# A lent fourth PSUM bank, later casts and a later batch 1 in a kernel of clustered attention and four experts

## The chip, the cores and the metric

The kernel runs on one core of one Trainium2 chip. The metric is the device time of one execution in microseconds (us). "Span" is the time from the first to the last recorded instruction of a profiled execution; it is about 1.8 us shorter than the device time. Engines are named as in the profile: PE is TensorE's matmuls, PEld its weight loads, DVE VectorE, ACT ScalarE, POOL GpSimd, SP the engine that issues most DMAs. The program gives each engine its own queue of instructions and makes engines wait for each other by semaphores; in the traces here an engine takes its queue in order (in pair 2 of the kernel before, an eviction that could have run at 175.7 us stood behind two casts until 178.32). PSUM is the memory that PE writes its sums to, in banks.

## The reference

Four batches, eight heads, 768 positions, head dimension 64. Queries and keys are put into one of 16 clusters per head, and attention is allowed only inside a cluster. The result goes through four experts, each a two-layer network, weighted by given probabilities.

```python
q_assign = np.argmax(np.einsum('bhsd,hcd->bhsc', q_n, c_n), axis=-1)
k_assign = np.argmax(np.einsum('bhsd,hcd->bhsc', k_n, c_n), axis=-1)
mask = q_assign[:, :, :, None] == k_assign[:, :, None, :]
scores = np.where(mask, scale * np.matmul(q, k.transpose(0, 1, 3, 2)), -1e9)
...                                        # softmax, then times v
x = attn_out.transpose(0, 2, 1, 3).reshape(3072, 512)
p = domain_probs / (domain_probs.sum(-1, keepdims=True) + 1e-09)
for e in range(4):                         # w1[e]: 512x1024, w2[e]: 1024x512
    h = np.maximum(x @ w1[e], 0.0)
    out += p[:, e:e + 1] * (h @ w2[e])
```

## The kernel before

The order of instructions is written by hand: a list of attention steps is woven with the expert matmuls of positions that are already done, and generators prepare the next batch (its "assignment": transposes, cluster scores, one-hots) at given step numbers. There are 72 attention steps to a batch (PER_B). The eight PSUM banks are shared out by tag:

```python
PS_BUFS = {"s": 2, "av": 1, "av2": 1, "mo": 3, "misc": 1}
def bank(tag, dtype=F32):
    n = 512 if dtype == F32 else 1024
    return psum.tile([128, n], dtype, name="ps_" + tag, tag=tag, bufs=PS_BUFS[tag])
```

A tile of a tag that is in use waits until its bank has been evicted. Three kinds of tile take "mo": the experts' hidden tiles (evicted by ACT), the experts' outputs (evicted by DVE), and the cluster scores of batches 2 and 3 (evicted by DVE).

```python
def expert(u, e):
    ...
        ph = bank("mo")
        ...  nc.tensor.matmul(ph[...], W1[e][...], xT[...], ...)          # L728
        nc.scalar.activation(ht, ph, ACT.Relu)                            # L734
    ...
        po = bank("mo")[:, c]
        ...  nc.tensor.matmul(po, hT[...], W2[e][...], ...)               # L747
        nc.vector.scalar_tensor_tensor(oacc[:, c], po, pap, oacc[:, c],   # L756
                                       op0=ALU.mult, op1=ALU.add)
```

The assignment of batches 2 and 3 handles four tiles (z = 0 is the first of two, z = 1 the second). Scores come in pairs, each of two groups of four fp32 matmuls, which the trace records as eight: a pair for each half of the heads, so pairs 1 and 2 belong to batch 2, pairs 3 and 4 to batch 3.

```python
        def casts(self):                       # DVE, two of 0.95 us per tile
            ...  dve(self.rows(...), self.all[...])                      # L387
        def scores_split(self, bank_tag):
            sc = bank(bank_tag)
            ...  nc.tensor.matmul(sc[32 * x:32 * x + 32, :QW], lhs, rhs, ...)   # L400
            ...  dve(self.sch[...], src[...])                            # L404
        ...
                t = 8 * y
                    put(t + 9 + j, lambda x=x, j=j: x.merge(j))          # POOL, L377
                put(t + 15, x.casts)
                at = 16 * (y // 2) + 24
            if b == 1:
                ...
            put(at, lambda x=x: x.scores_split("mo"))
            put(at + 2 + 6 * z, x.cross_scores)
            put(at + 5 + 6 * z, x.merge_scores)                          # POOL, L416
```

Batch 1 is prepared in another way, with transposes on PE into the single "misc" bank (L242), at the very start:

```python
    for b in range(1, B):
        gens.append(Paced(assigns(b), XSTEPS[b], PER_B * (b - 1) if b > 1 else S1 + 4,
                          PER_B * b - 2))
```

The softmax here doesn't subtract the row's maximum and nothing guards it: scores larger than these inputs give would overflow.

## Time and profile before

| | before |
|---|---|
| median of the first three runs | 482.76 us (482.57 to 483.82) |
| span | 480.9 us |
| PE busy | 467.7 us, 97% |
| DVE, ACT, POOL busy | 47%, 58%, 39% |
| granted TensorE clock in the profiled run | 1.0 throughout |

PE is the bound, and 13.2 us of its span are idle. The question is which of these the change can take. The lines that answer it (the table of what PE waited for, the windows by expert period and the timelines around the gaps) stand in the prediction. Read there: a line of a timeline is start, length, engine, source line, operation, output and inputs, count; in square brackets the idle time ahead of it and the instruction that ended it.

### The profile page before, as it was taken

To read this page: it belongs to the slowest core of one execution; us is meant where nothing else is said; L and a number is where in the kernel's file an instruction comes from. 1 tells how busy PE (TensorE), PEld (TensorE's weight loads), DVE (VectorE), ACT (ScalarE), POOL (GpSimd) and SP (SyncE) were. 2 spreads that over 40 slices of the span, in tenths; PEclk is the share of its full clock that TensorE was granted. 3 is DMA by queue.
4 is the path that set the end of the run, shared out by engine and by line. 5 is a ranking of instruction groups with operands and counts; after the bars stand their busy time and mean duration, and the time that the engine had idled before them with its cause. 6 is when DMAs were issued, how large, how long until landed. Compare 5 with 4: busy or idle time off the path is not lost.

```text
span 480.9 us, 11389 instructions
## 1 busy us (share of the span) xinstructions
PE 467.7 (97%) x4539; PEld 332.6 (69%) x4539; DVE 226.7 (47%) x561; ACT 277.4 (58%) x502; POOL 186.2 (39%) x301
## 2 busy tenths in 40 slices
PE   8998999999999989999999999999999999999997
PEld 4776777677775657767766776777666666766675
DVE  5864664222324562422234444431877867765112
ACT  5755656555564546656655665566566585574341
POOL 5937479273343667180145834000313222221000
PEclk9999999999999999999999999999999999999999
DMA  8999953824564743614565573312000100100101
GB/s 281 254 211 347 237 106 54 152 57 127 92 131 111 159 102 81 143 34 51 140 140 110 119 135 115 87 35 75 27 29 13 50 14 7 34 30 10 46 2 44
DMA packets 74557, 48.01 MB, mean 100 GB/s; under 512 B 50248, under 2 KB 69256, under 8 KB 74504
## 3 DMA queue, kind: packets, MB, share of 16 engines
q1 hardware_dynamic: 65256, 37.96, 31.8%
q0 software_dynamic: 8576, 9.25, 10.8%
q8 instruction: 35, 0.57, 0.5%
q10 hardware_dynamic: 672, 0.08, 0.1%
q14 instruction: 18, 0.15, 0.1%
HBM read 37.31 MB, written 6.30 MB: 91 GB/s over the span
## 4 chain that ended last, share of the span: by engine, by line
PE 85%; DMA 5%; DVE 3%; SPq 3%; POOL 2%; issue 1%; ACT 0%; POOLq 0%; DVEq 0%; ACTq 0%
PE ps_mo L728 32%; PE ps_mo L747 31%; PE ps_s L638 8%; PE ps_av L665 7%; DMA raw<-in_k_dram 4%; SPq L368 1%; PE ps_s L548 1%; DMA sct<-scs 1%; SPq L336 1%; PE ps_misc L242 1%; POOL t L377 1%; PE ps_mo L400 1%; PE ps_mo L242 1%; PE ps_misc L548 1%; DVE oacc L756 1%
## 5 line engine op out<-in xcount | busy, mean ns | idle before, releaser
L644 ACT ACTIVATE at<-ps_s 128x512 bf16<-128x512 f32 x252 | 147.9, 595 | 125.7 <-PE ps_s L638 110.5
L728 PE MATMUL ps_mo<-xT,w1b 128*128 128x256 bf16 (+1 forms) x1664 | 195.7, 264 | 0.0
L747 PE MATMUL ps_mo<-w2b,hT 128*128 128x512 bf16 (+1 forms) x776 | 189.9, 377 | 2.8 <-DVE oacc L756 2.8
L728 PEld LDWEIGHTS <-w1b 128*128 128x128 bf16 x1664 | 146.3, 98 | 24.1 <-issue 0.6
L734 ACT ACTIVATE hT<-ps_mo 128x512 bf16<-128x512 f32 x192 | 114.7, 598 | 60.7 <-PE ps_mo L728 57.6
L756 DVE SCALAR_TENSOR_TENSOR oacc<-ps_mo,psb,oacc 128x512 f32<-128x512 f32 (+1 forms) x73 | 54.2, 742 | 125.5 <-PE ps_mo L747 125.3
L747 PEld LDWEIGHTS <-hT 128*128 128x128 bf16 x776 | 67.2, 98 | 61.4 <-issue 6.6
L638 PE MATMUL ps_s<-qf,kf 80*128 80x256 bf16 (+1 forms) x456 | 82.8, 267 | 0.7 <-DVE t L252 0.4
L665 PEld LDWEIGHTS <-at 128*128 128x128 bf16 x1152 | 69.9, 97 | 15.3 <-issue 1.7
L665 PE MATMUL ps_av<-vx,at 128*128 128x65 bf16 x1152 | 80.3, 193 | 0.0
L651 POOL TENSOR_TENSOR at<-at,same 128x512 bf16<-128x512 bf16 x24 | 28.2, 1176 | 97.7 <-ACT at L644 82.2
L638 PEld LDWEIGHTS <-kf 80*128 80x128 bf16 x456 | 42.4, 98 | 20.7 <-issue 1.6
L565 DVE TENSOR_SCALAR same<-qf,late 128x256 bf16<-128x256 bf16 x144 | 39.1, 324 | 0.0
L377 POOL COPY t<-t 128x768 uint16<-128x768 uint16 x32 | 35.6, 1119 | 0.3 <-DMA t<-h 0.3
L651 DVE TENSOR_TENSOR at<-at,same 128x512 bf16<-128x512 bf16 x48 | 21.6, 451 | 25.9 <-ACT at L644 25.8
L358 POOL COPY h<-raw 128x768 uint16<-128x768 uint16 x16 | 13.0, 826 | 37.2 <-DMA raw<-in_q_dram 31.0
L754 DVE TENSOR_SCALAR oacc<-ps_mo,psb 128x512 f32<-128x512 f32 x18 | 13.5, 750 | 28.5 <-PE ps_mo L747 28.5
L361 POOL COPY h<-raw 128x768 uint16<-128x768 uint16 x16 | 13.0, 825 | 33.0 <-DMA raw<-in_q_dram 19.5
L336 POOL DMA_DIRECT2D kf<-oht x32 | 16.4, 526 | 22.9 <-DMA oht<-oh 14.2
L416 POOL COPY st<-sct 128x384 uint16<-128x384 uint16 x16 | 9.9, 662 | 37.5 <-DMA sct<-scs 37.2
L672 DVE RECIPROCAL zr<-ps_av 128x4 f32<-128x4 f32 (+1 forms) x50 | 8.9, 178 | 30.1 <-PE ps_av L665 30.0
L674 DVE TENSOR_TENSOR xn<-ps_av,zr 128x256 bf16<-128x256 f32 (+1 forms) x50 | 20.7, 414 | 1.7
(127 smaller groups left out, 284.8 us busy)
## 6 DMA issues: line engine op xcount, KB each, us to landing
raw<-in_v_dram SPq DMA_DIRECT2D x8, 768.0 KB, 5.6
out_dram<-oacc SPq DMA_DIRECT2D x23, 256.0 KB, 2.0
raw<-in_k_dram SPq DMA_DIRECT2D x7, 768.0 KB, 6.6
raw<-in_q_dram SPq DMA_DIRECT2D x6, 768.0 KB, 4.9
w1b<-in_moe_w_dram POOLq DMA_DIRECT2D x4, 1024.0 KB, 11.8
w2b<-in_moe_w_dram POOLq DMA_DIRECT2D x4, 1024.0 KB, 17.1
qf<-nos SPq DMA_DIRECT2D x2, 768.0 KB, 4.0
xT<-xn SPq DMA_TRANSPOSE x72, 2.4
```

Of the source, the lines that this page charges most:

```text
L336: (nc.gpsimd if self.b or self.i0 and self.g else nc.sync).dma_start(out=self.rows(slice(D, D + CL), j, r), in_=self.oht[p0:p0 + CL, :self.w])
L377: pool(self.all[:, y * w:(y + 1) * w].bitcast(U16)[:, z::2], self.t16[:, (2 * z + y) * w:(2 * z + y + 1) * w])
L565: nc.vector.tensor_scalar(same[:, x * 256:(x + 1) * 256], clusters(b)[:, g, w, k // 2, k % 2, :], key_nos[b % 2][:, g, 8 * i + 4 * (k // 2 ...
L638: nc.tensor.matmul(sp[:, x * n:(x + 1) * n], KF[b % 2][:K, h, r, i * 128:(i + 1) * 128], QF[b % 2][:K, h, rs[0]:rs[-1] + 1, w * 128:(w + 1 ...
L644: nc.scalar.activation(at, sp, ACT.Exp, scale=scale)
L651: (nc.gpsimd if n4 in POOL_STEPS else nc.vector).tensor_tensor(at, at, same_cluster(b, w, cur), op=ALU.mult)
L665: nc.tensor.matmul(av[:, h % 2, m, :], at[:, c0:c0 + 128], VX[b % 2][:, h, 2 * i + r, :], start=(first and x == 0 and m == 0), stop=(last ...
L674: nc.vector.tensor_tensor(xn[:, :nr].rearrange("p i j d -> p j i d"), av[:, :, :, :D], zr.broadcast_to([128, 2, nr, D]), op=ALU.mult)
L728: nc.tensor.matmul(ph[:, x * n:(x + 1) * n], W1[e][:, i, (f + x) * 128:(f + x + 1) * 128], xT[:, i, :], start=(i == 0), stop=(i == ND - 1))
L734: nc.scalar.activation(ht, ph, ACT.Relu)
L747: nc.tensor.matmul(po, hT[f // per][:, c0:c0 + 128], W2[e][:, f, c], start=(f == 0), stop=(f == NF - 1))
L756: nc.vector.scalar_tensor_tensor(oacc[:, c], po, pap, oacc[:, c], op0=ALU.mult, op1=ALU.add)
```

## The change

Its intent: give the crowded places a fourth bank, keep long DVE work from standing ahead of evictions, and start batch 1's preparation when its key load has landed. It has three parts.

```diff
+    spare, turns = False, 0
+    def ring():
+        nonlocal turns
+        turns += 1
+        return bank("misc" if spare and turns % 4 == 0 else "mo")
...
-        def scores_split(self, bank_tag):
-            sc = bank(bank_tag)
+        def scores_split(self):
+            sc = ring()
...
-                put(t + 15, x.casts)
+                put(t + 15 + 4 * z, x.casts)
...
-            put(at, lambda x=x: x.scores_split("mo"))
+            put(at, x.scores_split)
...
-            ph = bank("mo")
+            ph = ring()
...
-                po = bank("mo")[:, c]
+                po = ring()[:, c]
...
-        gens.append(Paced(assigns(b), XSTEPS[b], PER_B * (b - 1) if b > 1 else S1 + 4,
-                          PER_B * b - 2))
+        gens.append(Paced(assigns(b), XSTEPS[b], PER_B * (b - 1) if b > 1 else S1 + 7,
+                          PER_B * b - (2 if b > 1 else -2)))
...
+                spare = PER_B + 4 <= step < PER_B * (B - 1)
```

"misc" is lent between steps 76 and 216, when batch 1's transposes, its main user, are done. In the changed kernel all source lines below stand eight lines further down: L747 becomes L755, L756 becomes L764, L400 becomes L408, L242 becomes L250, L377 becomes L385, L387 becomes L395, L416 becomes L424.

More of the change, by code (lines that the diff above doesn't have):

```diff
@@ L894 @@
     for b in range(1, B):
-        gens.append(Paced(assigns(b), XSTEPS[b], PER_B * (b - 1) if b > 1 else S1 + 4,
-                          PER_B * b - 2))
+        gens.append(Paced(assigns(b), XSTEPS[b], PER_B * (b - 1) if b > 1 else S1 + 7,
+                          PER_B * b - (2 if b > 1 else -2)))
     def woven(works, upto):
+        nonlocal spare
         base, spent = step, 0.0
```

## The prediction

> **What bounds the kernel now.** I read the page's first part, then the table of who waited for whom with TensorE (PE) alone, then PE's timeline from end to end, then the timelines of VectorE (DVE), GpSimd (POOL) and the DMA queue (SP) around each gap in it.
>
> ```profile
> PE 467.7 (97%) x4539; PEld 332.6 (69%) x4539; DVE 226.7 (47%) x561; ACT 277.4 (58%) x502; POOL 186.2 (39%) x301
> ...
> PE ps_mo L747 <- DVE oacc L756: 2.8, 2, 2.0
> PE ps_misc L242 <- DMA raw<-in_k_dram: 2.0, 2, 1.6
> ...
> PE ps_mo L400 <- DVE oacc L756: 1.0, 1, 1.0
> PE ps_misc L242 <- DVE t L252: 0.5, 2, 0.3
> ```
>
> PE is idle 480.9 - 467.7 = 13.2 us of the span. A busy PE need not be a full one, so I checked the rate. Late in the chain, where experts run alone:
>
> ```profile
> 442.82 3.49 PE ps_mo L728 x32
> 446.31 3.45 PE ps_mo L747 x16
> ```
>
> That is 109 ns for a matmul of 256 columns and 216 ns for one of 512. In the middle of the kernel one expert period holds 32 of L728, 16 of L747, 12 of L638 (256 columns) and 24 of L665 (65 columns). The first three need 3.49 + 3.45 + 12 x 0.109 = 8.25 us, and the period is 9.01, which leaves 32 ns for each L665. So PE is at its pace there, and a fourth bank has nothing to take from an ordinary period. Four periods also hold a pair of score groups (L400). The windows below are, in order: ordinary, score pairs 1 to 4, ordinary. Columns: stretch, length, then busy us of PE, PEld, DVE, ACT and POOL.
>
> ```profile
> 129.83:138.84 9.01, 9.01 (x85) 6.59 (x84) 3.83 (x6) 5.56 (x10) 0.55 (x1) 1.00 0.76 168
> 138.84:150.60 11.76, 10.76 (x101) 6.85 (x100) 5.97 (x10) 5.56 (x10) 6.44 (x8) 1.00 0.51 81
> 168.62:181.19 12.57, 10.59 (x101) 7.06 (x100) 8.35 (x14) 5.56 (x10) 8.53 (x13) 1.00 0.47 115
> 253.26:263.80 10.54, 10.54 (x101) 6.92 (x100) 5.02 (x9) 5.56 (x10) 5.50 (x7) 1.00 0.60 100
> 281.82:293.29 11.47, 10.60 (x102) 7.00 (x100) 7.78 (x14) 5.56 (x10) 5.98 (x8) 1.00 0.44 55
> 302.30:311.31 9.01, 9.01 (x86) 6.59 (x85) 4.05 (x9) 5.56 (x10) 0.00 (x0) 1.00 0.28 41
> ```
>
> Pair 3 loses nothing (PE busy all of 10.54 us), so a pair costs 10.54 - 9.01 = 1.53 us of real work. The others should then also take 10.54, and lose 11.76 - 10.54 = 1.22, 12.57 - 10.54 = 2.03 and 11.47 - 10.54 = 0.93 us: 4.18 us together. The worst one, PE first and then DVE:
>
> ```profile
> 175.12 0.59 PE L747 MATMUL ps_mo<-w2b,hT 128*128 128x512 bf16 x2
> 175.65 1.50 PE L400 MATMUL ps_mo<-t,bdc 128*32 128x384 f32 x16
> 179.13 1.02 PE L747 MATMUL ps_mo<-w2b,hT 128*128 128x512 bf16 x4 [1.98 <-DVE oacc L756]
> ...
> 175.16 0.98 DVE L426 TENSOR_SCALAR oh<-oh 128x384 bf16<-128x384 bf16 x1
> 176.07 2.22 DVE L387 CAST qf<-t 64x1536 bf16<-64x1536 f32 x2
> 178.32 0.75 DVE L756 SCALAR_TENSOR_TENSOR oacc<-ps_mo,psb,oacc 128x512 f32<-128x512 f32 x1
> ```
>
> The ring "mo" has three banks. The first output of the expert, score group A and score group B fill all three within 2 us; the second output (L747 at 179.13) needs the first one's bank. Its eviction L756 could have run at about 175.7, but stood in DVE's queue behind the one-hot work and the two casts until 178.32. Pair 1 is alike, except that score group B is the one that waits, and the casts themselves waited for POOL's last merge (ended 145.29).
>
> The other stall of note is before batch 1's first transposes:
>
> ```profile
> 41.13 0.52 PE L242 MATMUL ps_misc<-ident,raw 128*128 128x128 f32 x3 [1.62 <-DMA raw<-in_k_dram]
> ...
> 45.54 0.55 PE L242 MATMUL ps_misc<-ident,raw 128*128 128x128 f32 x3 [0.34 <-DVE t L252]
> ```
>
> The load of that key tile was issued at 33.25 and landed at 41.0; PE came to it at 39.5. A third small one (0.18 us, at 59.9) is again a transpose waiting for the copy out of the single "misc" bank.
>
> **What the Trainium skill says.** "PSUM — Partial Sum Buffer", Specifications (TRN2): eight banks of 2 KiB a partition, so no ninth can be had. The kernel's pools take 2 + 1 + 1 + 3 + 1 = 8; the fourth has to be lent. "Perfetto Trace Analysis", Matmuls: independent groups should rotate through different banks, so that the eviction of one overlaps the next one's matmuls. The ordinary periods agree with three banks (9.01 of 9.01 us busy); the pairs show three run out. The same page, Identifying the Most-Contended Engine: matmul busy share is no good measure of closeness to the roof, hence my check by pace. "TensorE: Matmul & The Clock Gate", Back-to-back issue gap: N / 2.4 + 2.5 ns, which is 109 and 216 ns for 256 and 512 columns. The trace agrees to a nanosecond; the sustained 131 ns that the section names for 512 columns is not seen here.
>
> **The change, part by part.** It adds and removes no instruction. I compared the built programs: POOL's and SP's orders are identical, DVE's has the casts moved, and PE's has batch 1's transposes and scores moved; otherwise only bank names change.
>
> Fourth bank. From step 76 to 216 every fourth allocation of the expert and score matmuls takes "misc". In the built program pair 1 has first output, second output, A, B on banks 3, 2, 4, misc, and pairs 2 and 4 have first output, A, B, second output on 3, 4, 2, misc: four different banks each time. What held misc before is an expert hidden tile four allocations back, which ACT evicts in 0.6 us, so no wait replaces the old one. The next user of the first output's bank is the following expert's first tile, some 4 us later in pair 1 and 3.5 us in pair 2; L756 then has that long. Worth the 4.18 us in full.
>
> Casts. Those of each second tile move four paced steps later, behind the score copies and the next evictions. They last 2 x 0.95 us on DVE, which is 47% busy, and their data is needed only in the next batch. By themselves they would take most of the same stalls away; together with the bank the gain isn't counted twice. So 0 beyond the 4.18. They make it safer: in pair 1 L756 no longer queues behind a cast that waits for POOL.
>
> Batch 1 three steps later. In the new PE order three attention steps with two L747 each, some 0.77 us a piece, come ahead of the first transpose: 39.5 + 3 x 0.77 = 41.8, after the landing at 41.0. The 1.62 us go. The transposes are then less bunched on misc, so the 0.34 and 0.18 should go also: 2.14 at most. Against that, the last transposes and back-transposes move into steps where matmuls of an expert on "mo" stand closer. Going through the bank numbers by hand I find one tight place: a hidden tile reuses the bank of the one before it but for 0.8 us of other work, against 0.6 us of ACT plus its start, up to 0.3 us. I take 1.9 us net.
>
> Sum: 4.18 + 1.9 = 6.1 us; 482.76 - 6.1 = 476.7 us, ratio 0.987.
>
> **The rivals.** First: PE only trades the bank wait for a wait on POOL. Scores need the merged tiles. In pair 1 the last merge ends at 145.29 and group B starts about 0.75 us after 146.31, a margin of 1.8 us; in pair 2 it ends at 176.03 and group B starts near 176.4, a margin of 0.4 us. If the loads and DMA transposes didn't move forward with PE, the gain of pairs 2 and 4 would go: about 479.5 us. Against it: SP's queue is held at several points by evictions and attention outputs (at 113.7, 123.8, 153.5) that move with PE. So I keep the margin, but some tenths may be lost here.
>
> Second: batch 1's delay comes back. POOL runs without a break from 93.6 to 104.7 us after waiting for expert weights; it ends up later against PE by the 2 us that PE gains plus the shift of some 2 us. Batch 1's first attention matmul stands at 105.0; of what it needs, the values (cast until 101.6) come last, needed from about 107 on. The second half's one-hots are needed over 20 us later still, and the weights of the last expert landed by 93.5 for a use at 104.6. Slack is 4 us or more in each but the values, where it is just enough. If it fails the time is 478 to 480.
>
> Third: the gain is larger, because PE's idle time elsewhere shrinks too. It is 13.2 us, and 6.3 are named above; the start (1.2 us before the first matmul, and the setup to 30 us) and the end (2.4 us) aren't touched. Floor about 476.
>
> **Range and chances.** Full success is 476.4, the losses named bring it to 478 or so; 8 times in 10 within 475.7 and 478.8. Faster by over 2% needs 473.1, beyond all idle time that the change can reach: 0.03. Slower by over 2% would take a new stall of 16 us: 0.01. Within 2%: 0.96.
>
> **What would show it.** PE's table of waits no longer has L747 or L400 behind L756; the periods of the four pairs are all about 10.5 us, the ordinary ones still 9.01; DVE's casts come after the score copies. No PE wait for the key load near 41 us. PE idle in total near 7 us. I am wrong if the pair periods stay over 11 us, if score groups are seen to wait for POOL, if batch 1's first attention matmuls (about 103 us) wait for POOL or DMA, or if the time is outside the range while these waits are gone.

## More of the kernel before

The chain that ended last, share of the span by engine, was this:

```profile
PE 85%; DMA 5%; DVE 3%; SPq 3%; POOL 2%; issue 1%; ACT 0%; POOLq 0%; DVEq 0%; ACTq 0%
```

So 15% of the chain was not PE, although PE was busy 97% of the time: the chain goes through a wait's cause as far back as it takes, and so overstates what the wait costs.

## The result, and the profile after

| | before | after |
|---|---|---|
| median (range, runs) | 482.66 us (482.14 to 483.82, 4) | 476.25 us (475.74 to 476.53, 4) |
| span of the profiled run | 480.9 us | 474.5 us |
| granted clock of the profiled run | 1.0 | 1.0 |

The ratio is 0.9863 (95% interval 0.9843 to 0.9882). A ratio in this document is not quite the ratio of the medians quoted. The output is correct, the time is within 2% of before and 1.3 to 1.4% shorter; 476.7 was predicted.

First the page of the changed kernel: busy time by engine, then the chain that ended last.

```profile
PE 464.5 (98%) x4488; PEld 332.7 (70%) x4539; DVE 227.8 (48%) x561; ACT 277.3 (58%) x502; POOL 188.3 (40%) x301
...
PE 95%; DVE 1%; DMA 1%; issue 1%; ACT 1%; SPq 0%; ACTq 0%
```

The chain is now PE nearly throughout. The PE busy time of this line is not to be used: 51 of 4539 matmul records are missing from this trace, as the counts show (PEld has them all). A repeat of the same kernel (run e9_after below) has all records:

```profile
PE 467.5 (98%) x4539; PEld 333.3 (70%) x4539; DVE 227.6 (48%) x561; ACT 277.3 (58%) x502; POOL 186.9 (39%) x301
```

Its span is 474.7, so PE is idle for 7.2 us instead of 13.2, with the same busy time as before (467.7 there). In these two traces the whole gain is idle time that is gone. What PE waited for in the changed kernel (total us, times, longest):

```profile
PE ps_s L95 <- DVE blank L88: 1.2, 1, 1.2
PE ps_s L646 <- DVE t L260: 0.4, 1, 0.4
...
PE ps_mo L250 <- DMA raw<-in_k_dram: 0.3, 1, 0.3
```

Neither of the two lines with DVE's eviction (now L764) is left, nor the 2.0 us for the key load before L242 on "misc" (the 0.3 us above is another key load, at 5.7 us, where before has 0.2); the largest one is the start-up wait, which the change does not touch. The expert periods, here an ordinary one, pair 1 and pair 2 (length, busy us of PE, PEld, DVE, ACT, POOL, then clock, DMA share, GB/s):

```profile
146.72:155.73 9.01, 8.95 (x85) 6.59 (x84) 4.45 (x6) 5.56 (x10) 5.80 (x6) 1.00 0.47 114
136.17:146.72 10.55, 10.50 (x101) 6.92 (x101) 4.06 (x8) 5.56 (x10) 6.29 (x8) 1.00 0.57 88
164.74:175.73 10.99, 10.93 (x100) 7.04 (x100) 6.12 (x12) 5.56 (x10) 6.29 (x11) 1.00 0.48 96
```

The ordinary period is unchanged at 9.01, and pair 1 is at the floor of 10.54. Pair 2 is not: 0.45 us are missing. The timeline shows where. PE, then DVE, then POOL, around pair 2:

```profile
171.25 0.59 PE L755 MATMUL ps_mo<-w2b,hT 128*128 128x512 bf16 x2
171.77 1.95 PE L408 MATMUL ps_mo<-t,bdc 128*32 128x384 f32 x16
173.65 1.04 PE L755 MATMUL ps_misc<-w2b,hT 128*128 128x512 bf16 x4
```

```profile
172.86 0.73 DVE L764 SCALAR_TENSOR_TENSOR oacc<-ps_mo,psb,oacc 128x512 f32<-128x512 f32 x1
173.52 1.94 DVE L412 COPY scs<-ps_mo 128x384 uint16<-128x384 uint16 x4
...
178.49 1.91 DVE L395 CAST qf<-t 64x1536 bf16<-64x1536 f32 x2
```

```profile
169.44 1.16 POOL L424 COPY st<-sct 128x384 uint16<-128x384 uint16 x2 [6.67 <-DMA sct<-scs]
170.50 2.32 POOL L385 COPY t<-t 128x768 uint16<-128x768 uint16 x2
```

The second output is now written to "misc" (173.65) straight after the score groups, while DVE is still copying the scores, and the casts follow 3 us after that. This is what the fourth bank and the later casts were for. But the 16 score matmuls took 1.95 us instead of 1.50. The second eight, which begin at 172.44, read the tile that POOL's last merge (L385) completes only at 172.82: in the single records of the trace, the last four of them begin at 172.88 and later, while in before they follow within 0.34 us. No idle time is printed: the records that began at 172.77 are said to last 0.49 us each, past the start of the next at 172.88, and the view merges all 16 into one line. A stall inside such a group shows only as a group that is longer than its like.

To see where the 6.4 us came from, I took the start of the same attention matmul (the k-th of L638, L646 in the changed kernel) in both traces, and how much earlier it is:

| stretch | gained, changed kernel | gained, repeat | predicted |
|---|---|---|---|
| batch 1's preparation (36 to 78 us) | 2.63 | 2.64 | 1.9 |
| pair 1 | 1.21 | 1.21 | 1.22 |
| pair 2 | 1.58 | 2.03 | 2.03 |
| pair 4 | 0.92 | 0.51 | 0.93 |
| sum of the pairs | 3.71 | 3.75 | 4.18 |
| sum | 6.34 | 6.39 | 6.1 |

The start of the first of these attention matmuls itself differs between the traces, by up to 0.9 us (12.45 to 13.33), so that the sums differ a little from the difference of the spans. Where PE started late, as in e2 below (0.9 us), and batch 1 stood in its old place, it made the delay up at the key load: that wait ends at a landing and not a given time after PE's own work.

### The profile page after: what moved, and what is told of

Same layout as the page of the kernel before. It is cut to its first block, busy times and chain, and to the rows that moved or that the text cites. A ratio compares the mean times of both kernels' runs of the same rounds, so it can differ in the third digit from the quotient of the medians.

```text
span 474.5 us, 11333 instructions
## 1 busy us (share of the span) xinstructions
PE 464.5 (98%) x4488; PEld 332.7 (70%) x4539; DVE 227.8 (48%) x561; ACT 277.3 (58%) x502; POOL 188.3 (40%) x301
## 4 chain that ended last, share of the span: by engine, by line
PE 95%; DVE 1%; DMA 1%; issue 1%; ACT 1%; SPq 0%; ACTq 0%
PE ps_mo L736 31%; PE ps_mo L755 29%; PE ps_s L646 10%; PE ps_av L673 8%; PE ps_misc L755 5%; PE ps_misc L736 4%; PE ps_s L556 1%; DMA raw<-in_q_dram 1%; PE ps_misc L250 1%; PE ps_mo L408 1%; PE ps_mo L250 1%; PE ps_misc L556 1%; PE ps_mo L275 1%; PE ps_misc L275 1%; DVE oh L295 0%
## 5 line engine op out<-in xcount | busy, mean ns | idle before, releaser
L736 PE MATMUL ps_mo<-xT,w1b 128*128 128x256 bf16 (+1 forms) x1464 | 172.8, 264 | 0.0
L755 PE MATMUL ps_mo<-w2b,hT 128*128 128x512 bf16 (+1 forms) x621 | 157.8, 376 | 2.3
L742 ACT ACTIVATE hT<-ps_mo 128x512 bf16<-128x512 f32 x168 | 100.4, 598 | 58.2 <-PE ps_mo L736 56.4
L755 PEld LDWEIGHTS <-hT 128*128 128x128 bf16 x776 | 67.0, 98 | 57.5 <-issue 3.1
L764 DVE SCALAR_TENSOR_TENSOR oacc<-ps_mo,psb,oacc 128x512 f32<-128x512 f32 (+1 forms) x62 | 45.9, 740 | 113.9 <-PE ps_mo L755 109.3
L646 PE MATMUL ps_s<-qf,kf 80*128 80x256 bf16 (+1 forms) x456 | 83.0, 267 | 1.0 <-DVE t L260 0.4
L646 PEld LDWEIGHTS <-kf 80*128 80x128 bf16 x456 | 42.4, 98 | 20.8 <-issue 1.7
L385 POOL COPY t<-t 128x768 uint16<-128x768 uint16 x32 | 36.3, 1144 | 0.0
L755 PE MATMUL ps_misc<-w2b,hT 128*128 128x512 bf16 x104 | 26.5, 379 | 0.0
L736 PE MATMUL ps_misc<-xT,w1b 128*128 128x256 bf16 (+1 forms) x200 | 26.2, 268 | 0.0
L424 POOL COPY st<-sct 128x384 uint16<-128x384 uint16 x16 | 10.7, 713 | 31.1 <-DMA sct<-scs 31.1
```

What stands on the lines that cost most here:

```text
L385: pool(self.all[:, y * w:(y + 1) * w].bitcast(U16)[:, z::2], self.t16[:, (2 * z + y) * w:(2 * z + y + 1) * w])
L646: nc.tensor.matmul(sp[:, x * n:(x + 1) * n], KF[b % 2][:K, h, r, i * 128:(i + 1) * 128], QF[b % 2][:K, h, rs[0]:rs[-1] + 1, w * 128:(w + 1 ...
L736: nc.tensor.matmul(ph[:, x * n:(x + 1) * n], W1[e][:, i, (f + x) * 128:(f + x + 1) * 128], xT[:, i, :], start=(i == 0), stop=(i == ND - 1))
L755: nc.tensor.matmul(po, hT[f // per][:, c0:c0 + 128], W2[e][:, f, c], start=(f == 0), stop=(f == NF - 1))
```

## The experiments

All times are medians over runs that agree within 1%, in the fast state; all kernels gave the right result unless it is said otherwise. The runs came in three calls, each on another chip and with its own runs of before (medians 483.08, 482.96 and 484.01). "Pair periods" are the lengths of the four expert periods that hold score pairs, from the profiled run; 10.54 is the floor, and before had 11.76, 12.57, 10.54 and 11.47.

The theory: the stalls in the pairs are DVE's late evictions, for want of a bank and because the casts stand ahead of them; the one at 41 us is a key load. The first rival: it is POOL that sets the pairs. Others: two of the parts do the same work; batch 1's delay is paid for later.

### One part alone

**e1_bank**: the fourth bank alone. Against the changed kernel:

```diff
-                put(t + 15 + 4 * z, x.casts)
+                put(t + 15, x.casts)
...                                           # and batch 1 at S1 + 4, to PER_B * b - 2
```

> The fourth bank alone; casts and batch 1 stand as in the kernel before. Theory A (a lack of banks for the three tiles of a score pair): the stalls behind the oacc eviction go although the casts still hold DVE; pairs 1, 2 and 4 fall from 11.76, 12.57 and 11.47 us to about 10.6, 11.0 and 10.5, and 10.54 is the floor; time 3.7 us below before, about 479.0. Rival B (the casts that hold DVE are what costs, the bank is worth little): pairs stay over 11.3 us, time within 1 us of before. The stall at the key load (41 us) stays in both.

Measured: 478.26 us (478.06 to 478.37, 6 runs), ratio 0.9895 (0.987 to 0.9919). Pair periods 10.55, 10.63, 10.54, 10.55. The bank alone takes 4.07 of the 4.18 us.

**e2_casts**: the later casts alone, with three banks.

```diff
-                spare = PER_B + 4 <= step < PER_B * (B - 1)
+                spare = False
...                                           # and batch 1 at S1 + 4, to PER_B * b - 2
```

> The later casts alone, three banks. Theory A in its strict form (a fourth bank is needed): pairs stay near 11.5 us or above, time within 1.5 us of before. Rival B (either one is enough, since the eviction of the first output then runs before its bank is asked for again): the same pairs as with the bank alone, 10.6, 11.0 and 10.5 us, time about 479.0, 3.7 us below before. I hold B for likelier by the gaps: with the casts gone the eviction would end at about 176.9 in pair 2 of the kernel before, and PE asks for the bank at 177.2.

Measured: 478.59 us (478.26 to 478.86, 6), ratio 0.9902 (0.9877 to 0.9927). Pair periods 10.55, 10.54, 10.54, 10.66: 4.05 of the 4.18 us. With the casts out of the way DVE evicts the first output in time, and three banks are enough. PE, then DVE, at pair 2:

```profile
175.71 1.04 PE L755 MATMUL ps_mo<-w2b,hT 128*128 128x512 bf16 x4
```

```profile
174.76 0.73 DVE L764 SCALAR_TENSOR_TENSOR oacc<-ps_mo,psb,oacc 128x512 f32<-128x512 f32 x1
```

The eviction ends at 175.49, before PE comes to the second output. The two parts are worth the same 4 us, and each of them takes nearly all of it without the other.

**e3_batch1**: the later batch 1 alone.

```diff
-                put(t + 15 + 4 * z, x.casts)
+                put(t + 15, x.casts)
...
-                spare = PER_B + 4 <= step < PER_B * (B - 1)
+                spare = False
```

> Batch 1 three steps later alone. Theory: it saves the three stalls of the transposes, 2.6 us from start to start (1.78 + 0.51 + 0.35), which the idle column shows as 2.14; the four score pairs stay at 11.76, 12.57, 10.54 and 11.47 us; time about 480.0. Rival: it saves 1.9 as predicted, the rest of the 6.4 being due to the fourth bank early in its use: 480.8.

Measured: 480.27 us (479.62 to 481.25, 6), ratio 0.9937 (0.9909 to 0.9966). By the alignment it gains 2.63 us up to 78 us, as the changed kernel does there. The pairs did not stay as expected: they took 11.14, 14.15, 10.54 and 11.59 us. Pair 1 lost 0.61 us of its stall by this part alone: its casts wait for POOL's last merge, which ended 1.64 us ahead of the first scores (141.99 to 143.63) where before it was 1.03 (145.28 to 146.31), and the eviction behind the casts ran that much sooner. Pair 2 took 14.15 us instead of 12.57, which is taken up below under "the clock".

**e8_casts_batch1**: the changed kernel without the bank, and beside it **e9_after**, the changed kernel once more.

```diff
-                spare = PER_B + 4 <= step < PER_B * (B - 1)
+                spare = False
```

> Casts and batch 1 moved, but three banks: the changed kernel without its fourth bank. Theory (either cure of the pairs is enough, as runs with one alone showed 10.54 to 10.66): same time as the changed kernel within 0.5 us, pairs at 10.5 to 11.0. Rival: with batch 1 moved the margins on POOL are thinner and the fourth bank is needed as a cushion: at least one pair over 11.0 and 0.7 us or more behind the changed kernel.

> The changed kernel once more, as it is, to see whether pair 2 again loses about 0.45 us (period 10.99 in its first profile) and to have it on the same chip as the next runs. Theory: the loss comes from POOL's last merge, which ends with some tenths of jitter, so pair 2 lies anywhere from 10.55 to 11.1. Time near 476.2.

Measured: 476.16 us (475.71 to 476.24, 4), ratio 0.9857 (0.9835 to 0.9878), against 475.91 (475.72 to 476.52, 5), ratio 0.9853 (0.9832 to 0.9874). The intervals lie over each other. Once the casts are late, the fourth bank is worth nothing that can be measured here. The pairs were 10.55, 10.54, 10.54, 10.66 without it and 10.54, 10.54, 10.55, 10.96 with it.

### The lost tenths: POOL's last merge

**e4_merge_order**: the changed kernel, with POOL's merge of a second group's scores one step later. In POOL's queue the scores of pair 1's second group stand among the tile merges that pair 2 needs: with two of the four behind them in the changed kernel, and with one here.

```diff
-            put(at + 5 + 6 * z, x.merge_scores)
+            put(at + 5 + 7 * z, x.merge_scores)
```

> The changed kernel, with POOL's merge of the second score tile's scores behind three of the four last tile merges instead of behind two. Theory: in the changed kernel pair 2 still loses 0.45 us (period 10.99, not 10.54) because its second score group waits for POOL's last merge, which stands behind a merge that waits for a DMA transpose; here pair 2 falls to 10.54 to 10.6, and the span to about 474.1 against 474.5. Rival: the 0.45 us is due to something else (DVE or the banks), and pair 2 stays at 10.99. Timing will hardly resolve it; the period in the trace will.

Measured: 475.87 us (475.8 to 476.56, 5), ratio 0.985 (0.9822 to 0.9877). All four pairs are at the floor: 10.54, 10.55, 10.55, 10.54. PE, then POOL, at pair 2:

```profile
171.78 1.50 PE L408 MATMUL ps_mo<-t,bdc 128*32 128x384 f32 x16
```

```profile
169.53 1.14 POOL L424 COPY st<-sct 128x384 uint16<-128x384 uint16 x2 [5.51 <-DMA sct<-scs]
170.58 1.05 POOL L385 COPY t<-t 128x768 uint16<-128x768 uint16 x1
```

Here POOL has one tile merge left behind the score merge instead of two, it ends at 171.63, and the same 16 matmuls that begin at the same time as in the changed kernel take 1.50 us. So the merge was the cause of the 0.45 us. **e12_merge_again** is the same kernel. It was run on another chip.

> The changed kernel with POOL's merge order mended, once more. The changed kernel lost 0.46 us in pair 2 in one profile and 0.41 in pair 4 in the other, where its second score group met POOL's last merge; the mended one had all four pairs at 10.54 or 10.55. Theory: again all four at 10.54 to 10.56, since the last merge ends over 1 us earlier. Rival: the first clean profile was chance, and a pair at 10.7 or more appears. Time 475.5 to 476.2.

Measured: 476.01 us (475.75 to 476.56, 5), ratio 0.9842 (0.9815 to 0.9868); pairs 10.55, 10.54, 10.54, 10.54. So eight pairs of eight are at the floor, against six of eight in the two traces of the changed kernel. That alone is little (e5 below has four of four without this edit), but all the traces kept say the same. Leaving out e7, whose groups stand apart, they hold 52 pairs. In four of them (pair 2 of the changed kernel, of e6 and of e11, pair 4 of e9) the last merge ended after the second eight had begun, by 0.34 to 0.53 us, and in just these four the eight took longer. In the other 48 it ended 0.10 us or more ahead. That settles the first rival. The times (475.87 and 476.01 against 476.25 and 475.91) do not tell the two apart: single runs of each spread over 0.8 us.

### How far batch 1 has to move

**e5_batch1_2steps** and **e6_batch1_6steps**: two and six steps later instead of three.

```diff
-    ... if b > 1 else S1 + 7, PER_B * b - (2 if b > 1 else -2)))       # changed kernel
+    ... if b > 1 else S1 + 6, PER_B * b - (2 if b > 1 else -2)))      # e5
+    ... if b > 1 else S1 + 10, PER_B * b - (2 if b > 1 else -5)))     # e6
```

> The changed kernel with batch 1 two steps later instead of three. Theory (PE must fill the time until the key tile lands at 41.0 us, at 0.77 us a step from 39.35): it comes at 40.9, so the wait for the load is 0 to 0.3 us, and the time within 0.4 us of the changed kernel. Rival (what counts is the wider spacing of the transposes, not the landing): a part of the 0.51 and 0.35 us gaps behind VectorE's copies stays, though the load's wait is gone.

> Batch 1 six steps later. The key tile has landed in any case, so theory says nothing more is won; what was feared in the prediction (batch 1's values and one-hot rows late on POOL) should now show: its value casts then run behind the start of batch 2's copies, and PE waits for them or for the one-hot rows near 103 to 110 us, time 1 to 6 us above the changed kernel. Rival: there is slack enough on POOL and the time is that of the changed kernel within 0.5 us.

Measured: e5 476.58 us (476.31 to 477.52, 4), ratio 0.9871; e6 477.59 us (476.62 to 477.68, 5), ratio 0.9883. e5 lies 0.67 us above the repeat of the same call (475.91), a little more than the 0.4 expected. By the alignment it gains 2.17 us in batch 1's stretch, 0.46 less than three steps do. One line of its timeline accounts for most of that (the rest is 0.08 us that the first transpose still waits for the key load):

```profile
57.28 0.61 PE L736 MATMUL ps_mo<-xT,w1b 128*128 128x128 bf16 x8 [0.23 <-ACT hT L742]
```

A hidden tile waits for ACT to evict the one before it from the same bank: a place of the kind that the prediction called "one tight place". The line before it starts at 56.78 and is normally followed after 0.11 us, so 57.28 - 56.78 - 0.11 = 0.39 us are lost here, not the 0.23 printed. It is there with two steps and not with three. With six steps the net gain is 1.85 us, and two new gaps make up most of the loss. At 61.8 us PE loses 0.56: its transpose of an attention output waits for DVE, which works on batch 1's one-hots until 61.17 and only then evicts that output. At 48.5 us it loses 0.19, at a transpose that waits for the "misc" bank. The second rival (POOL's values near 105 us come too late) did not show in any of the three: e6's time, 1.7 us above the repeat, lies in the range expected, but PE waits for nothing near 103 to 110 us. And e6's pair 2 took 11.14 us, and its L408 group 2.09, which is POOL's merge again. So three steps are near the best of these, and the loss for six comes from elsewhere than was feared.

### Is it the number of banks?

**e7_apart**: the kernel before with three banks, casts and batch 1 in their old places, but the second group of each score pair four steps later.

```diff
-            put(at, lambda x=x: x.scores_split("mo"))
+            put(at + 4 * z, x.scores_split)                               # and spare = False
```

> The kernel before (three banks, casts and batch 1 in place) with the second score group of each pair four paced steps later than the first, so that no two fall together. Theory (three tiles within 2 us on three banks make the shortage): pair 1's stall goes, since the bank is asked for only after the eviction at 148.0; pair 2 keeps at most 0.6 us, pair 4 less; about 3.5 us of the 4.2 are saved, time about 479. Rival (the shortage is there for each score group alone): stalls of 1 us and more stay, time over 481.

Measured: 479.46 us (479.04 to 479.82, 6), ratio 0.9912 (0.989 to 0.9934). Each pair is now spread over two expert periods of 9.90 us (its groups of eight start at 174.24 and 182.06, for instance, and take 0.85 us each), and no score group waits for a bank. A pair costs 2 x (9.90 - 9.01) = 1.78 us like this, 0.25 more than the 1.53 of a closed pair, so that the pairs gain 3.2 us by the alignment and not 4.2. The shortage before was of three tiles falling within 2 us, with the evictions behind casts; it was not a shortage of banks in general.

### Is DVE's queue still on the path?

**e10_long_stall** is the kernel before with one query cast of each query tile of batch 2 done twice (the same result); **e11_long_after** the changed kernel with the same edit.

```diff
-                for r in range(2):
+                for r in (0, 1) if self.t else (0, 0, 1):
```

> The kernel before with one cast of the query tiles of batch 2 done twice (same data): 0.95 us more of VectorE work ahead of the eviction in pairs 1 and 2, nothing on PE. Theory 1 (the stalls are VectorE's delay, one for one): pairs 1 and 2 grow by about 0.95 us each, to 12.7 and 13.5. Theory 2, on top (a stall of PE of 3 us or more is followed by some us at about half the granted clock, as one profile showed at 176 to 180 us and as the runs of the kernel before at a mean clock of 0.996 suggest): most runs have a mean clock of 0.996 or less, and the time rises by 1.9 + 1.7 us or more, to 486 or above. Rival to 2: the clock dips are chance, a third of the runs has them as before, and the median is near 484.7.

> The same doubled casts in the changed kernel. Theory: VectorE's casts are no longer ahead of an eviction that PE waits for, and the eviction has time until the bank comes round again, so they cost nothing: pairs at 10.54 to 11.0, time within 0.4 us of the changed kernel (476.0), mean clock 1.0 in every run. Rival: the later casts now delay something else on VectorE, 0.5 to 2 us more.

Measured: e10 486.44 us (486.15 to 488.61, 6), ratio 1.0067 (1.0041 to 1.0092); e11 476.42 us (475.86 to 476.62, 4), ratio 0.9847 (0.9821 to 0.9874). In before, pair 1 loses 0.80 us more and pair 2's stall grows by 1.14, from 1.98 to 3.12 us, each about a cast's length (0.95). Pair 4, whose casts are not doubled, loses another 0.65 us, again by what stands ahead of the eviction: POOL's copy of the scores (L416), which waits for a DMA and which DVE's one-hots need, starts 2.32 us ahead of the first output's last matmuls (289.13 to 291.45) instead of 2.98 (285.35 to 288.33), and the eviction follows 0.64 us later against them. In the changed kernel the extra casts cost nothing that shows: its four stretches gained 2.64, 1.21, 1.56 and 0.92. That DVE's order was the cause in before, and is off the path after the change, is shown by this pair of runs.

### The clock

e3's profile has a dip of PE's granted clock behind pair 2's stall, which before's profile, with the same stall, has not. Columns: stretch, length, PE busy (matmuls), clock, DMA share, GB/s. First e3, then e10:

```profile
175.00:176.00 1.00, 0.17 (x1) 1.00 0.27 34
176.00:177.00 1.00, 1.00 (x4) 0.61 0.67 226
177.00:178.00 1.00, 1.00 (x8) 0.50 1.08 407
178.00:179.00 1.00, 1.00 (x3) 0.50 1.45 298
179.00:180.00 1.00, 1.00 (x7) 0.68 0.82 105
180.00:181.00 1.00, 1.00 (x15) 1.00 0.06 12
```

```profile
180.00:181.00 1.00, 0.43 (x2) 1.00 0.86 324
181.00:182.00 1.00, 1.00 (x5) 0.58 1.06 397
182.00:183.00 1.00, 1.00 (x8) 0.50 0.45 106
183.00:184.00 1.00, 1.00 (x3) 0.50 0.92 183
184.00:185.00 1.00, 1.00 (x9) 0.72 0.05 12
```

After the stall PE has the full clock for about half a microsecond, then some 3.4 us at half of it, and counts as busy all the while: the cost shows in the matmul counts (3 to 9 in a microsecond instead of 15) and not in any idle time. The missing share of the clock in the four slices that are under 1.00 adds up to 0.39 + 0.50 + 0.50 + 0.32 = 1.71 us in e3, and to 0.42 + 0.50 + 0.50 + 0.28 = 1.70 in e10. The time agrees: in e10 the stretch of pair 2 and the period behind it is 2.81 us longer than in before, 1.14 of which is the longer stall; the dip cost the other 1.67.

The skill's page "TensorE: Matmul & The Clock Gate", section "What's actually happening", describes such a mechanism: the clock falls to a half after an idle window of about 3.4 us and comes back after a busy one of that length. The length of the dip agrees (3.4 us). The stall ahead of it was shorter here: 3.12 us in e10, where all six runs show the dip (mean clock 0.996 or less), and 1.97 us in e3. In before it is 1.98 us, and 13 of its 31 runs in the three calls had a mean clock of 0.996, which is what one dip makes of it (1 - 1.7 / 480). Those average 484.58 us, the other 18 average 482.65, so by this estimate a dip costs 1.9 us. Of e3's six runs one is at 0.996; of the 54 runs of the kernels without so long a stall (all but before, e3 and e10) none is under 0.999. I did not see before's dip in a trace, since its profiled run has none; that it falls behind pair 2's stall is taken over from e3, which has the same stall. Why the same stall is followed by a dip in some runs and not in others stays open, and so does whether the 1.5 us of fp32 score matmuls ahead of the stall, which use 32 columns of the array, count towards the idle window.

So there is a second gain that no idle time of the profile shows: 13/31 x 1.93 = 0.8 us of the mean. It would account for the ratios of the repeats (0.985, that is 7 us) being a little better than the 6.4 us between the two traces, neither of which holds a dip.

## Why the prediction was right

The time (476.25 against 476.7) and the range were right, and for most of the reasons given. By its steps:

- **The bound and the pace.** Right. Ordinary periods stayed at 9.01 us, and PE's idle time is 7.2 us where "near 7" was said.
- **The fourth bank, 4.18 us "in full".** The mechanism is right (e1 alone: 4.07), and the waits behind L756 are gone. The changed kernel delivers 3.71, and 3.75 in the repeat. What is missing is one event of 0.4 to 0.5 us, in pair 2 of one trace and in pair 4 of the other.
- **The first rival, POOL.** "Some tenths may be lost here" is what came, and e4 shows the cause. The prediction put the margin in pair 2 at 0.4 us (by before's records it is 0.29, from 176.03 to 176.32) and held that it would keep. It came out at -0.39 us in one trace and at +0.42 in the repeat, where pair 4 had -0.34. So one of the prediction's own signs of being wrong, score groups that wait for POOL, did come, at the size of some tenths that it had allowed for, and pair 2's 10.99 us is not the "about 10.5" that it named.
- **The casts, "0 beyond the 4.18".** Right, and stronger than was said: e2 shows that they take nearly all of the stalls by themselves, and e8 that the bank adds nothing to them.
- **Batch 1, "1.9 us net", "2.14 at most".** The mechanism was right and the size off: it was 2.63. This term was taken from the idle column, 1.62 + 0.34 + 0.18. That column counts from the end of the matmul before, which is modelled and too late. From start to start, before's three gaps are larger. The line before the first gap, a line of the same kind with no gap after it, and the one after that:

```profile
39.23 0.28 PE L665 MATMUL ps_av<-vx,at 128*128 128x65 bf16 x4
...
42.14 0.28 PE L665 MATMUL ps_av<-vx,at 128*128 128x65 bf16 x4
42.26 0.60 PE L747 MATMUL ps_mo<-w2b,hT 128*128 128x512 bf16 x2
```

  With no wait the next matmul starts 0.12 us after L665's, though L665 is said to last 0.28; before the first transpose it took 41.13 - 39.23 = 1.90. The gap is 1.78 and not 1.62. The same for the other two gives 0.51 and 0.35: 2.64 together, against 2.63 measured. (The prediction's "PE came to it at 39.5" has the same error: 39.23 + 0.12 is 39.35.) (The skill's page "Perfetto Trace Analysis", section "Summary: the profiler window per engine type", says that TensorE's end is an estimated one; in this trace the difference is 0.16 to 0.17 us at each of these gaps.) The pairs were sized by periods, from start to start, and in e4, where no merge is late, they came out to within 0.02 us of their sum (4.16). The "up to 0.3 us" lost at a tight place was not lost with three steps; e5 shows it with two.
- **The second rival, batch 1's delay coming back.** It did not, with three steps. With six some of it does, in another place than was named.
- **The third, a floor of about 476.** Right: the best of the variants is at 475.9.
- **Not foreseen:** the clock dips. The errors of the two sizes (-0.5 and +0.7) nearly cancelled, so that it is partly luck that the time came within half a microsecond of the one predicted; the dips are a gain beside both, which the first runs of before (median 482.66) hardly show and the later ones (medians up to 484.01) do.

The best version is the changed kernel with the score merge one step later (e4, e12): 475.87 and 476.01 us. Its pairs are all at the floor, but its gain over the changed kernel is smaller than the spread of single runs.

## What to carry to other kernels

Size a stall from start to start against the same sequence where it runs without a stall, not from the idle column of a pipelined engine, and look for groups that are longer than their like. When a bank comes free too late, look at what stands ahead of its eviction in the evicting engine's queue before adding banks: here moving two casts by four steps did what a fourth bank did, and both together did no more. Stalls of 2 to 3 us of TensorE were followed here, in some runs or in all, by a clock dip that cost another 1.7 to 1.9 us, so such stalls are worth removing first.

## What the Trainium skill lacked or had wrong

- "Perfetto Trace Analysis", Summary: the profiler window per engine type: it says that TensorE's end is estimated, but not what follows for reading gaps. Here the idle column understated three gaps by 0.16 to 0.17 us each: 2.14 us by the column, 2.64 from start to start, 2.63 measured. In pairs 1, 2 and 4 it was 0.22, 0.05 and 0.06 us.
- "TensorE: Matmul & The Clock Gate", What's actually happening: the idle window of about 3.4 us reads as a threshold. Here the clock fell to 0.50 after a recorded gap of 1.97 us, and 13 of 31 runs of a kernel with such a gap (1.98 us) had the mean clock of 0.996 that one dip gives; with 3.12 us 6 of 6 had it or less. A dip cost 1.7 to 1.9 us.
- The same page, Back-to-back issue gap: the sustained 131 ns that it names for 512 columns was not seen; 16 such matmuls took 3.45 us, 216 ns each.
- No page says that a stall inside a run of like matmuls can leave no idle time at all, since the estimated end of one lies past the start of the next: 16 score matmuls of 1.50 us took 1.95 when POOL's merge came late, and no gap was recorded.
